# Letting either addition of a bundle run on GpSimd, in a kernel whose exponentials are shared by two engines

## The chip, the cores and the metric

The kernel runs on one core of a Trainium2 chip. The time is device microseconds of that core. The median before is 694.38 us.

## The reference

Two attention blocks read the same input x (2048 x 512) and their outputs are mixed by a gate. Block A is softmax attention with 32 heads of width 16, block B is linear attention with the feature map phi. Each has a fused weight for Q, K, V and an output weight.

```python
def _A_ref(x, wqkv, wo):
    ...
    scores = jnp.einsum("bhqd,bhkd->bhqk", q, k) * (Dh ** -0.5)
    p = _softmax(scores, axis=-1)
    o = jnp.einsum("bhqk,bhkd->bhqd", p, v)
    ...
def _B_ref(x, wqkv, wo):
    ...
    phi = lambda t: jnp.where(t > 0, t + 1, jnp.exp(t)) + 1e-6
    pq, pk = phi(q), phi(k)
    kv = jnp.einsum("bhsd,bhse->bhde", pk, v)
    ...
g = _sigmoid((x * gate_w).sum(-1, keepdims=True))
return g * a + (1 - g) * b
```

Block A needs 32 x 2048 x 2048 exponentials. They are most of the work.

## The kernel before

**Units and rounds.** Block A is cut into 32 rounds (`rounds`): a group of eight heads, a chunk of 512 queries, and one half of the eight heads. A round has 64 units (`NU`). A unit is one head, 128 keys and 512 queries: one matmul of scores into one PSUM bank (128 x 512), the exponential of it, and then the product of the exponentials with V, which is summed in an accumulator bank over the round.

**Two ways to an exponential.** ScalarE takes two or three units at a time (an instruction of 128 x 1024 or 128 x 1536, L2021) and writes bf16 to the tile PT. Or a unit is *claimed* (`claim`): VectorE evicts the scores (L1536), scaling and adding a bias so that the 16-bit integer it writes, read as a float16, is a piecewise linear exponential. To make that precise, three versions of it are summed, whose integers differ by the constants `STEPS` (0, 342, 683). So four claimed units form a *bundle* (`NTRI` = 4): their four evictions go to one buffer of the tile DP (`NB` = 13 buffers, 128 x 2048 each), and when it is full it is closed (`close_tri`, `try_close`): two *additions* of a constant to the whole buffer write the second and the third version to two further buffers. TensorE then makes three products for a claimed unit, with V scaled by a weight, where a ScalarE unit takes one.

**Who adds.** An addition on VectorE is a 16-bit add of a scalar (L1586). On GpSimd it is a 32-bit add of a constant held twice in 32 bits (L1579, the constant in the tile `step`). Only the second addition of a bundle (`z == NG4 - 1`) is given to GpSimd, and only if the bundle is full, all of one round, that round is the one ScalarE is in and isn't the last, and over `POOL_LEFT` = 22 of its units are unclaimed. Which engine an addition uses is fixed when it is queued. Before a GpSimd addition is issued, a VectorE addition must have been issued since the last one (`last_add`, `boost`), and the GpSimd addition waits for its result by a semaphore (`sync`).

**The plan.** All instructions are put in order by a planner written in Python, which runs when the kernel is built. It keeps an estimated time for each engine and estimated ready times of each buffer. VectorE's waiting work is a list of items with priorities (0 and 1 for evictions and most others, 3 for additions). `pump` picks the next one for VectorE, `pool_go` offers items to GpSimd, and `est_start` says when an operation could begin; for a VectorE operation that doesn't read PSUM it adds the times in which GpSimd is expected to run (`pool_runs`). On the chip each engine simply runs its list in order, with semaphores between dependent instructions.

**What decides on a claim.** After each group of scores the planner claims a unit if a PSUM bank is free, a buffer is free (`can_claim`), and the work that waits for VectorE (`dve_load`) is under 3.7 to 4 us. In a group of scores the third bank goes to a claimed unit if one can be claimed, or else, if it is free, to ScalarE as a third unit. While a closed bundle lacks buffers for its additions, the start of another is held back (`MOST_OPEN` = 0).

**Around it.** Projections, block B and the output are *steps* with a target, a count of exponential groups (`cur_g`: units given to ScalarE, divided by three). Targets are multiples of `GPR`, groups a round. TensorE fills idle time with matmuls on a constant tile (`fill`) where its share of useful work falls below `MAC_LOW`.

Of the kernel before, what the change touches and what calls it, by code (L numbers as in the profile page):

```python
# [9 lines left out]
ALU = mybir.AluOpType  # L10
# [3 lines left out]
I32 = mybir.dt.int32  # L14
I16 = mybir.dt.int16
U16 = mybir.dt.uint16

STATS = {}
# [12 lines left out]
STEPS = (0, 342, 683)  # L31
NG4 = len(STEPS)
# [172 lines left out]
def d_sb(n, rate=1.0):  # L205
    return 0.15 + n * 1.042e-3 * rate
# [6 lines left out]
def bass_gated_mix__mha_block__linear_attn_block__prompt_kernel(  # L213
# [27 lines left out]
    pairs_ = [(t8, qc) for t8 in range(NT8 - 2) for qc in range(NQC)] + LAST_ORDER  # L241
    KV0, KV1 = 1.0, 1.2
    PRE_T = 5
    PRE_GAP = 8
    OUT_GAP = 4

    with ExitStack() as es:
        _cnt = [0]

        def SB(shape, dt, name):  # L250
            _cnt[0] += 1
            return es.enter_context(nc.sbuf_tensor(f"{name}_{_cnt[0]}", list(shape), dt))
# [48 lines left out]
        NTU = 512 * NTRI  # L301

        DP = SB([128, NB, NTU], BF16, "DP")
# [5 lines left out]
        rbc = SB([128, 512], FP32, "rbc")  # L309
        dev = SB([128, 2, 128], FP32, "dev")  # L310
        flag = SB([128, 1], I32, "flag")
        step2 = SB([128, 2], I16, "step")
        epool = SB([128, 2, 512], BF16, "epool")
        KVbd = SB([128, NCC, 128], BF16, "KVbd")
        Zsel = SB([128, NCC, 8], BF16, "Zsel")
# [37 lines left out]
        DV = _Eng("dve", SEM("s_dve"))  # L353
# [44 lines left out]
        r_step = R("step")  # L398
# [19 lines left out]
        def est_start(E, reads, writes):  # L418
            t = E.t
            for res in list(reads) + list(writes):  # L420
                if res.we is not E:
                    t = max(t, res.tw + LAT)
                elif not E.ordered:
                    t = max(t, res.tw + SELF_T)
            for res in writes:
                t = max(t, res.tr + LAT)
            if E is DV and not any(res in r_bank for res in reads):
                for a, b in pool_runs:
                    if a <= t < b:
                        STATS["blk"] = STATS.get("blk", 0) + b - t  # L430
                        t = b
            return t

        pool_runs = collections.deque(maxlen=4)
        POOL_SOON = 0.3
        POOL_PASS = 1.0
        last_add = [[], False]
        boost = [False]
        POOL_TT = 1.3
        POOL_V = 0.9  # L440
        POOL_ADD = 1.97
        EVERY = 1
        POOL_LEFT = 22
        OT_POOL = 1
        V2_POOL = 0

# [16 lines left out]
        def blocked(it, reads, writes):  # L463
            return blocker(it, reads, writes) is not None

        def emit_item_op(it, sync=[]):
            fn, reads, writes, dur, after, *on_pool = it.ops.popleft()
            for res in reads:
                res.pend -= 1
            for res in writes:  # L470
                res.pend -= 1
                res.pw -= 1
            if not it.ops:
                items.remove(it)
            if on_pool:
                _emit(PO, fn, reads + sync, writes, on_pool[0])
                pool_runs.append((PO.t - on_pool[0] + 0.08, PO.t + 0.08))
            else:
                _emit(DV, fn, reads, writes, dur)
            if after is not None:  # L480
                after()

        def pool_go(sync=None):

            for it in sorted(items, key=lambda i: i.seq):
                o = it.ops[0]
                if len(o) > 5 and not blocked(it, o[1], o[2]) and est_start(PO, o[1], o[2]) <= DV.t + POOL_SOON:
                    if not last_add[1] and any(x.prio == 3 and len(x.ops[0]) == 5 and not blocked(x, x.ops[0][1], x.ops[0][2])
                                               for x in items):
                        boost[0] = True  # L490
                        return
                    boost[0] = last_add[1] = False
                    STATS["pool"] = STATS.get("pool", 0) + 1
                    emit_item_op(it, last_add[0])
                    return

        def settle(reads, writes):
# [51 lines left out]
        def due_now(it):  # L549
            return of_round.get(it.seq, NR) <= acc_round[0] < act_round[0]  # L550

        def pump(now, look=0.25):
            try_close()
            pool_go()
            while items and DV.t <= now + look:
                best = None
                for it in items:
                    o = it.ops[0]
                    if len(o) > 5 or blocked(it, o[1], o[2]):
                        continue  # L560
                    st = est_start(DV, o[1], o[2])
                    wait = st - DV.t
                    key = (wait > (WAIT_BANK if it.prio <= 1 else 0.12), -1 if it.prio == 3 and (boost[0] or (RUSH and it.ops[0][5:] == () and due_now(it))) else it.prio, st, it.seq)
# [6 lines left out]
                emit_item_op(best[1])  # L570
                pool_go()

        def dve_load(now):
            return max(0.0, DV.t - now) + sum(o[3] for it in items for o in it.ops)

        def flush_items():
            while items:
# [135 lines left out]
        op(PO, lambda: nc.gpsimd.memset(step2[:], STEPS[2]), writes=[r_step], dur=0.1)  # L713
        op(PO, lambda: nc.gpsimd.memset(identb[:], 0.0), writes=[r_ident])
        op(PO, lambda: nc.gpsimd.affine_select(out=identb[:], in_=identb[:], compare_op=ALU.not_equal,
                                               fill=1.0, base=0, pattern=[[-1, 128]], channel_multiplier=1),
# [770 lines left out]
            return r + 1  # L1487

        MIN_LEFT = 14
        MIN_LEFT_LAST = 18  # L1490

        def can_claim(now, js):

# [58 lines left out]
        LAZY = 1  # L1552
        EARLY_ADDS = 1
        MOST_ADDS = 20
        MOST_OPEN = 0
        CLAIM_FREE_OPEN = 2

        def try_close():

            while closing:  # L1560
                i, us, zs = closing[0]
                z = len(zs) + 1
                if z == NG4:
# [12 lines left out]
                mine_, out_ = r_DP[i][0:len(us)], r_DP[i2][0:len(us)]  # L1576
                if (EVERY and z == NG4 - 1 and n == NTU and ntri[0] % EVERY == 0 and us[0][0] == us[-1][0] < NR - 1
                        and us[0][0] == act_round[0] and NU - len(taken[us[0][0]]) > POOL_LEFT):
                    push(3, [(lambda z=z, i2=i2, y=DP[:, i, 0:n].bitcast(I32), n=n: nc.gpsimd.tensor_tensor(  # L1579
                        DP[:, i2, 0:n].bitcast(I32), y, step2[:].bitcast(I32).to_broadcast([128, n // 2]), ALU.add),  # L1580
                        mine_ + [r_step], out_, 0.0, None, POOL_ADD)])
                else:
                    def added(out_=out_):
                        last_add[:] = [out_, True]
                        boost[0] = False
                    push(3, [(lambda z=z, i2=i2, y=y, n=n: nc.vector.tensor_single_scalar(DP[:, i2, 0:n].bitcast(I16), y, STEPS[z], ALU.add),  # L1586
                              mine_, out_, d_sb(n, 0.25), added)])
                of_round[iseq[0]] = us[0][0]
                for k, (r, u) in enumerate(us):
                    add_products(i2, z, k, r, u)  # L1590
            return True


        Q_OFF = -4
        GPR = 15.2
        B0 = 0.8
        B1 = 21
        chains = []

# [213 lines left out]
        FILL_AHEAD = 0.9  # L1813
# [499 lines left out]
```

## Time and profile before

| | |
|---|---|
| median of 3 runs | 694.38 us (693.92 to 694.49) |
| the profiled execution | 693.24 us, of which the span is 691.4 us |
| ScalarE busy | 677.6 us, 98% of the span |
| TensorE busy | 670.5 us, 97% |
| VectorE busy | 624.7 us, 90% |
| GpSimd busy | 249.6 us, 36% |
| granted TensorE clock | 1.000 |

In the rows below PE is TensorE, ACT ScalarE, DVE VectorE, POOL GpSimd, PEld TensorE's weight loads. A row of a group has the line, the engine, the operation, what it writes and reads, shapes and count; then the busy time in us and the mean duration in ns; then the engine's idle time before these instructions and what ended it. A row of the timeline has the start and the duration in us. In a row of a table by stretches, each engine has its busy time and, in brackets, its number of instructions. Neighbouring instructions of one engine overlap a little, so a group's busy time is less than its count times its mean.

### The profile page before, as it was taken

The numbers are of one execution on the slowest core, as the hardware profiler recorded it, in microseconds if no ns is written. First come the engines' busy times: TensorE is split into PE (matmuls) and PEld (weight loads), VectorE is DVE, ScalarE is ACT, GpSimd is POOL, SyncE is SP. The second block draws the span as 40 slices with busy tenths as digits, with TensorE's granted clock in tenths as the row PEclk, the third lists the DMA queues.
The fourth block names the chain that finished last, engine by engine and source line by source line (L and its number), as shares of the span: only waits on it lengthen the run. The fifth ranks groups of instructions, "written<-read, shape, count | busy, mean of one in ns | idle before, by whom it ended". The sixth has DMA issues, their size and how long they took to land.

```text
span 691.4 us, 19104 instructions
## 1 busy us (share of the span) xinstructions
PE 670.5 (97%) x8082; PEld 203.0 (29%) x8084; DVE 624.7 (90%) x1066; ACT 677.6 (98%) x718; POOL 249.6 (36%) x148
## 2 busy tenths in 40 slices
PE   8999999999999999999999999999999999999997
PEld 4322222333223322333232223233222322222223
DVE  4699999898888996998999999999999999999995
ACT  6999999999999999999999999999999999999996
POOL 4033434533235342343323444444334343334400
PEclk9999999999999999999999999999999999999999
DMA  9800101010010012100002010010201201010111
GB/s 228 233 3 14 21 2 32 4 24 13 1 34 3 14 21 63 34 2 18 18 14 51 1 29 15 11 33 11 39 18 23 54 21 41 18 34 24 35 28 46
DMA packets 44815, 22.95 MB, mean 33 GB/s; under 512 B 33976, under 2 KB 40568, under 8 KB 44728
## 3 DMA queue, kind: packets, MB, share of 16 engines
q1 hardware_dynamic: 42712, 20.12, 12.9%
q10 hardware_dynamic: 2016, 1.57, 0.8%
q8 instruction: 66, 1.08, 0.7%
q14 instruction: 21, 0.17, 0.1%
HBM read 8.00 MB, written 2.10 MB: 15 GB/s over the span
## 4 chain that ended last, share of the span: by engine, by line
ACT 80%; PE 15%; DVE 4%; issue 0%; POOL 0%; ACTq 0%; POOLq 0%
ACT PT L2021 78%; PE ps L664 15%; ACT epool L948 2%; DVE DP L1536 2%; DVE DP L1586 1%; DVE epool L951 0%; DVE DP L2123 0%; DVE oraw L1277 0%; DVE xT L1881 0%; DVE phi L953 0%; DVE KT L837 0%; PE ps L671 0%; DVE OB L1076 0%; DVE DP L2128 0%; DVE flag L2133 0%
## 5 line engine op out<-in xcount | busy, mean ns | idle before, releaser
L2021 ACT ACTIVATE PT<-ps 128x1024 bf16<-128x1024 f32 (+1 forms) x678 | 666.5, 1216 | 1.8 <-PE ps L664 1.4
L1536 DVE TENSOR_SCALAR DP<-ps 128x512 int16<-128x512 f32 x612 | 401.7, 683 | 38.1 <-PE ps L664 34.5
L1579 POOL TENSOR_TENSOR DP<-DP,step 128x1024 int32<-128x1024 int32 x116 | 225.9, 1947 | 349.2 <-DVE DP L1586 220.0
L664 PE MATMUL ps<-Qpad,KT 32*128 32x512 bf16 x2048 | 273.7, 384 | 12.7 <-ACT PT L2021 8.2
L664 PE MATMUL ps<-DP,Vaug 128*32 128x512 f16 x1831 | 199.9, 384 | 1.3 <-DVE oraw L1277 0.9
L664 PE MATMUL ps<-PT,Vaug 128*32 128x512 bf16 x1425 | 176.3, 385 | 1.0 <-DVE Vaug L892 0.5
L664 PEld LDWEIGHTS ps<-Qpad,KT 32*128 32x128 bf16 x2048 | 68.6, 91 | 278.8 <-ACT PT L2021 250.5
L1586 DVE TENSOR_SCALAR DP<-DP 128x2048 int16<-128x2048 int16 x190 | 127.4, 686 | 0.2
L664 PEld LDWEIGHTS ps<-DP,Vaug 128*32 128x32 bf16 x1831 | 48.4, 94 | 65.1 <-issue 37.7
L664 PEld LDWEIGHTS ps<-PT,Vaug 128*32 128x32 bf16 x1425 | 41.6, 94 | 54.0 <-issue 40.5
L664 PE MATMUL ps<-warm 128*32 128x512 bf16 (+1 forms) x381 | 56.3, 385 | 1.1 <-POOL step L713 1.1
L1265 POOL TENSOR_TENSOR OT<-oraw,rbc 128x512 bf16<-128x512 f32 x12 | 15.3, 1274 | 56.4 <-DMA rbc<-oraw 28.6
L664 PE MATMUL ps<-xT,wA 128*32 128x512 bf16 x432 | 32.7, 384 | 0.0
L948 ACT ACTIVATE epool<-ps 128x512 bf16<-128x512 f32 x32 | 24.2, 756 | 0.0
L1277 DVE COPY oraw<-ps 128x512 f32<-128x512 f32 x31 | 21.1, 681 | 0.6 <-PE ps L664 0.5
L664 PE MATMUL ps<-wB,xT 128*32 128x512 bf16 x256 | 19.1, 384 | 0.1
L664 PE MATMUL ps<-xT,wB 128*32 128x512 bf16 x256 | 19.1, 383 | 0.0
L664 PEld LDWEIGHTS ps<-warm 128*32 128x32 bf16 (+1 forms) x381 | 14.3, 97 | 15.0 <-issue 12.0
L664 PE MATMUL ps<-woA,OT 128*32 128x512 bf16 (+1 forms) x226 | 18.6, 383 | 0.0
L837 DVE CAST KT<-ps 128x512 bf16<-128x512 f32 (+1 forms) x16 | 10.7, 667 | 6.3 <-PE ps L664 6.3
L953 DVE SCALAR_TENSOR_TENSOR phi<-ps,epool 128x512 bf16<-128x512 f32 x24 | 16.2, 675 | 0.0
L664 PE MATMUL ps<-wA,xT 128*128 128x128 bf16 x192 | 14.5, 220 | 0.0
(106 smaller groups left out, 242.8 us busy)
## 6 DMA issues: line engine op xcount, KB each, us to landing
rbc<-oraw SPq DMA_DIRECT2D x16, 256.0 KB
OT<-in_A_x_dram SPq DMA_DIRECT2D x4, 512.0 KB, 7.2
Qpad<-Qs SPq DMA_DIRECT2D x124, 16.0 KB, 1.8
oraw<-oraw SPq DMA_DIRECT2D x60, 32.0 KB, 1.9
wA<-in_A_wqkv_dram SPq DMA_DIRECT2D x1, 1536.0 KB, 7.6
wB<-in_B_wqkv_dram SPq DMA_DIRECT2D x1, 1536.0 KB, 8.5
out_dram<-outt SPq DMA_DIRECT2D x12, 128.0 KB, 1.7
phi<-in_A_x_dram ACTq DMA_DIRECT2D x3, 256.0 KB, 6.3
```

The source lines that it names most:

```text
L664: return lambda: nc.tensor.matmul(o, lhsT=l, rhs=r, start=start, stop=stop, skip_group_check=sg)
L837: push(1, [(lambda: nc.vector.tensor_copy(KT[:, par, c0:c1], src), [r_bank[b]], [r_KT[par][t]], d_psum(n), None)])
L948: op(AC, lambda: nc.scalar.activation(epool[:, s, :], bank_ap(b), ACT.Exp), reads=[r_bank[b]], writes=[r_e[s]], dur=0.6, issue=0.48)
L953: (lambda: nc.vector.scalar_tensor_tensor(out=dst, in0=bank_ap(b), scalar=0.0, in1=epool[:, s, :], op0=ALU.max, op1=ALU.add), [r_bank[b], ...
L1265: push(1, [(lambda: (nc.gpsimd if on_pool else nc.vector).tensor_tensor(OT[:, t8, 512 * qc:512 * (qc + 1)], oraw[:, 0, :], rbc[:], ALU.mul ...
L1277: push(0, [(lambda: nc.vector.tensor_copy(oraw[:, half, :], acc), [r_acc], [r_oraw[half]], d_psum(512), evicted)])
L1536: push(0 if in_group else 1, [(lambda: nc.vector.tensor_scalar(DP[:, i, 512 * k:512 * (k + 1)].bitcast(I16), bank_ap(b), FRAC - Y_BIAS4, Y ...
L1579: push(3, [(lambda z=z, i2=i2, y=DP[:, i, 0:n].bitcast(I32), n=n: nc.gpsimd.tensor_tensor(DP[:, i2, 0:n].bitcast(I32), y, step2[:].bitcast ...
L1586: push(3, [(lambda z=z, i2=i2, y=y, n=n: nc.vector.tensor_single_scalar(DP[:, i2, 0:n].bitcast(I16), y, STEPS[z], ALU.add), mine_, out_, d ...
L2021: op(AC, lambda p0=p0, b0=b0, n=n: nc.scalar.activation(PT[:, 512 * p0:512 * p0 + n], ps[:, 512 * b0:512 * b0 + n], ACT.Exp, scale=LN2 / F ...
```

## The change

Any addition of a full bundle may now run on either engine, and the choice falls when it is issued. The tile of constants holds both. `pool_go` offers such an addition to GpSimd unless it is due (`due_now`: ScalarE has left its round and the products have reached it), and stands back if GpSimd has run until lately (`YIELD`) and VectorE has another operation on SBUF that could start at once. `pump` lets VectorE take one that isn't due only if GpSimd is occupied for `POOL_WAIT` = 0.7 us more. `port_free` makes GpSimd's estimated start wait for VectorE's last operation on SBUF; the semaphore wait (`sync`) is gone. A waiting addition counts with 0.4 of its duration in VectorE's load (`ADD_W`). With `MOST_OPEN` = 1 a new bundle may be opened while one closed bundle still lacks buffers. Ten numbers of the plan are changed too.

```diff
-    PRE_GAP = 8
+    PRE_GAP = 5
...
-        step2 = SB([128, 2], I16, "step")
+        steps = SB([128, 4], I16, "step")
...
+            elif E is PO:
+                t = max(t, port_free[0])
             return t
...
+        POOL_WAIT = 0.7
+        port_free = [0.0]
+        boost = [None]
+        ADD_W = 0.4
+        YIELD = 1.2
+        YIELD_SOON = 0.2
...
-        def emit_item_op(it, sync=[]):
+        def emit_item_op(it, pool=None):
...
-            if on_pool:
-                _emit(PO, fn, reads + sync, writes, on_pool[0])
+            if len(other) > 1 and pool is None:
+                pool = est_start(PO, reads, writes) + other[0] < est_start(DV, reads, writes) + dur
+            if other and (len(other) == 1 or pool):
...
+                _emit(PO, fn, reads, writes, other[0])
...
             else:
+                if not any(res in r_bank for res in reads):
+                    port_free[0] = est_start(DV, reads, writes) + dur - 0.03
                 _emit(DV, fn, reads, writes, dur)
...
-                    if not last_add[1] and any(x.prio == 3 and len(x.ops[0]) == 5 and not blocked(x, x.ops[0][1], x.ops[0][2])
-                                               for x in items):
-                        boost[0] = True
+                    if len(o) > 6 and due_now(it):
+                        continue
+                    if boost[0] is None and PO.t > DV.t - YIELD:
+                        boost[0] = next((x for x in items if not any(res in r_bank for res in x.ops[0][1]) and len(x.ops[0]) != 6 and x is not it
+                                         and (len(x.ops[0]) == 5 or due_now(x)) and not blocked(x, x.ops[0][1], x.ops[0][2])
+                                         and est_start(DV, x.ops[0][1], x.ops[0][2]) <= DV.t + YIELD_SOON), None)
+                    if boost[0] is not None:
                         return
...
-                    if len(o) > 5 or blocked(it, o[1], o[2]):
+                    if len(o) == 6 or blocked(it, o[1], o[2]):
+                        continue
+                    if len(o) > 6 and not due_now(it) and PO.t < DV.t + POOL_WAIT:
                         continue
...
-            return max(0.0, DV.t - now) + sum(o[3] for it in items for o in it.ops)
+            return max(0.0, DV.t - now) + sum(o[3] * (ADD_W if len(o) > 6 else 1) for it in items for o in it.ops)
...
-        op(PO, lambda: nc.gpsimd.memset(step2[:], STEPS[2]), writes=[r_step], dur=0.1)
+        for z in range(1, NG4):
+            op(PO, lambda z=z: nc.gpsimd.memset(steps[:, 2 * z - 2:2 * z], STEPS[z]), writes=[r_step], dur=0.1)
...
-        MIN_LEFT_LAST = 18
+        MIN_LEFT_LAST = 20
...
-        MOST_OPEN = 0
+        MOST_OPEN = 1
...
+                ops = (lambda z=z, i2=i2, y=y, n=n: nc.vector.tensor_single_scalar(DP[:, i2, 0:n].bitcast(I16), y, STEPS[z], ALU.add),
+                       mine_, out_, d_sb(n, 0.25), None)
+                if n == NTU:
+                    ops = (ops[0], mine_ + [r_step], out_, ops[3], None, POOL_ADD, lambda z=z, i2=i2, y=DP[:, i, 0:n].bitcast(I32), n=n: nc.gpsimd.tensor_tensor(
+                        DP[:, i2, 0:n].bitcast(I32), y, steps[:, 2 * z - 2:2 * z].bitcast(I32).to_broadcast([128, n // 2]), ALU.add))
+                push(3, [ops])
...
-        Q_OFF = -4
-        GPR = 15.2
-        B0 = 0.8
+        Q_OFF = 0
+        GPR = 14.8
+        B0 = 0.4
...
-        OVER = 0.12
+        OVER = 0.15
...
-        MAC_LOW = 0.45
+        MAC_LOW = 0.43
...
-        LATE = 7
+        LATE = 8
```

More of the change, by code (lines that the diff above doesn't have):

```diff
@@ L435, in bass_gated_mix__mha_block__linear_attn_block__prompt_kernel @@
         POOL_SOON = 0.3
-        POOL_PASS = 1.0
-        last_add = [[], False]
-        boost = [False]
+        POOL_WAIT = 0.7
[4 more added lines that the diff above has]
+        YIELD_SOON = 0.2
         POOL_TT = 1.3
@@ L441, in bass_gated_mix__mha_block__linear_attn_block__prompt_kernel @@
         POOL_ADD = 1.97
-        EVERY = 1
-        POOL_LEFT = 22
         OT_POOL = 1
@@ L464, in blocked @@
             return blocker(it, reads, writes) is not None
-        def emit_item_op(it, sync=[]):
-            fn, reads, writes, dur, after, *on_pool = it.ops.popleft()
+        def emit_item_op(it, pool=None):
+            fn, reads, writes, dur, after, *other = it.ops.popleft()
             for res in reads:
@@ L474, in emit_item_op, with pool_go @@
                 items.remove(it)
-            if on_pool:
-                _emit(PO, fn, reads + sync, writes, on_pool[0])
-                pool_runs.append((PO.t - on_pool[0] + 0.08, PO.t + 0.08))
-            else:
+            if len(other) > 1 and pool is None:
+                pool = est_start(PO, reads, writes) + other[0] < est_start(DV, reads, writes) + dur
+            if other and (len(other) == 1 or pool):
+                if len(other) > 1:
+                    fn = other[1]
+                    STATS["pool"] = STATS.get("pool", 0) + 1
+                _emit(PO, fn, reads, writes, other[0])
+                pool_runs.append((PO.t - other[0] + 0.08, PO.t + 0.08))
+            else:
+                if not any(res in r_bank for res in reads):
+                    port_free[0] = est_start(DV, reads, writes) + dur - 0.03
                 _emit(DV, fn, reads, writes, dur)
+            if it is boost[0]:
+                boost[0] = None
             if after is not None:
                 after()
-        def pool_go(sync=None):
+        def pool_go():
             for it in sorted(items, key=lambda i: i.seq):
@@ L487, in pool_go @@
                 if len(o) > 5 and not blocked(it, o[1], o[2]) and est_start(PO, o[1], o[2]) <= DV.t + POOL_SOON:
-                    if not last_add[1] and any(x.prio == 3 and len(x.ops[0]) == 5 and not blocked(x, x.ops[0][1], x.ops[0][2])
-                                               for x in items):
-                        boost[0] = True
+                    if len(o) > 6 and due_now(it):
[5 more added lines that the diff above has]
+                    if boost[0] is not None:
                         return
-                    boost[0] = last_add[1] = False
-                    STATS["pool"] = STATS.get("pool", 0) + 1
-                    emit_item_op(it, last_add[0])
+                    emit_item_op(it, True)
                     return
@@ L562, in pump @@
                     wait = st - DV.t
-                    key = (wait > (WAIT_BANK if it.prio <= 1 else 0.12), -1 if it.prio == 3 and (boost[0] or (RUSH and it.ops[0][5:] == () and due_now(it))) else it.prio, st, it.seq)
+                    key = (wait > (WAIT_BANK if it.prio <= 1 else 0.12), -1 if it is boost[0] else it.prio, st, it.seq)
                     if best is None or key < best[0]:
@@ L569, in pump @@
                     return
-                emit_item_op(best[1])
+                emit_item_op(best[1], False)
                 pool_go()
         def dve_load(now):
-            return max(0.0, DV.t - now) + sum(o[3] for it in items for o in it.ops)
+            return max(0.0, DV.t - now) + sum(o[3] * (ADD_W if len(o) > 6 else 1) for it in items for o in it.ops)
         def flush_items():
@@ L1576, in try_close @@
                 mine_, out_ = r_DP[i][0:len(us)], r_DP[i2][0:len(us)]
[L1577 to L1587, printed above, removed]
+                ops = (lambda z=z, i2=i2, y=y, n=n: nc.vector.tensor_single_scalar(DP[:, i2, 0:n].bitcast(I16), y, STEPS[z], ALU.add),
[4 more added lines that the diff above has]
+                push(3, [ops])
                 of_round[iseq[0]] = us[0][0]
```

## The prediction, made before the change was run

> **What bounds the kernel now.** I read the page first: busy shares, then the chain that ended last.
>
> ```profile
> PE 670.5 (97%) x8082; PEld 203.0 (29%) x8084; DVE 624.7 (90%) x1066; ACT 677.6 (98%) x718; POOL 249.6 (36%) x148
> ...
> ACT 80%; PE 15%; DVE 4%; issue 0%; POOL 0%; ACTq 0%; POOLq 0%
> ```
>
> ScalarE is busy through 98% of a span of 691.4 us and holds 80% of the chain. So the time is the number of exponentials that ScalarE computes itself, times what one costs. Every unit that VectorE claims is one fewer for ScalarE. The groups of instructions, with shapes kept apart, give both prices:
>
> ```profile
> L2021 ACT ACTIVATE PT<-ps 128x1024 bf16<-128x1024 f32 x598 | 568.0, 1167 | 1.1 <-PE ps L664 0.9
> L2021 ACT ACTIVATE PT<-ps 128x1536 bf16<-128x1536 f32 x80 | 118.9, 1585 | 0.7 <-PE ps L664 0.5
> ...
> L1536 DVE TENSOR_SCALAR DP<-ps 128x512 int16<-128x512 f32 x612 | 401.7, 683 | 38.1 <-PE ps L664 34.5
> L1586 DVE TENSOR_SCALAR DP<-DP 128x2048 int16<-128x2048 int16 x190 | 127.4, 686 | 0.2
> ...
> L1579 POOL TENSOR_TENSOR DP<-DP,step 128x1024 int32<-128x1024 int32 x116 | 225.9, 1947 | 349.2 <-DVE DP L1586 220.0 <-DVE DP L1536 129.1
> L1265 POOL TENSOR_TENSOR OT<-oraw,rbc 128x512 bf16<-128x512 f32 x12 | 15.3, 1274 | 56.4 <-DMA rbc<-oraw 28.6 <-DVE DP L1586 14.4 <-DVE Vaug L892 5.8
> ```
>
> 598 x 2 + 80 x 3 = 1436 units on ScalarE, 612 on VectorE, together the 2048 of 32 rounds. 612 units are 153 bundles of four, with 306 additions: 190 on VectorE, 116 on GpSimd. One unit costs ScalarE 568.0 / 1196 = 0.475 us. It costs VectorE 401.7 / 612 = 0.656 us for the eviction, and an addition 127.4 / 190 = 0.671 us. The eviction row shows VectorE's only large wait, 38.1 us. To see whether VectorE is full where it matters I read the timeline:
>
> ```profile
> 106.79 1.32 DVE L1536 TENSOR_SCALAR DP<-ps 128x512 int16<-128x512 f32 x2
> 108.03 0.68 DVE L869 TENSOR_SCALAR Qs<-ps 128x512 bf16<-128x512 f32 x1
> 108.63 1.32 DVE L1536 TENSOR_SCALAR DP<-ps 128x512 int16<-128x512 f32 x2
> 109.86 0.34 DVE L1250 RECIPROCAL rraw<-rsum 128x32 f32<-128x32 f32 x1
> 110.17 0.69 DVE L1536 TENSOR_SCALAR DP<-ps 128x512 int16<-128x512 f32 x1
> 110.78 0.68 DVE L1586 TENSOR_SCALAR DP<-DP 128x2048 int16<-128x2048 int16 x1
> ```
>
> No gap stands between these rows. So ScalarE and VectorE are full together, and the split between them sets the time. The 80 three-wide exponentials say the same: outside the start, ScalarE takes a third unit when a bank was free and no claim could be made. GpSimd is the engine with room, 36% busy.
>
> **The change, part by part.**
>
> *How many additions can move.* Today only the second addition of a bundle goes to GpSimd, under five conditions, and it waits for a VectorE addition. Afterwards either may go. The timeline of GpSimd shows the room (first and last of 128 rows from 40 us on):
>
> ```profile
> 40.09 1.89 POOL L1579 TENSOR_TENSOR DP<-DP,step 128x1024 int32<-128x1024 int32 x1 [30.48 <-DVE DP L1536]
> 43.75 1.89 POOL L1579 TENSOR_TENSOR DP<-DP,step 128x1024 int32<-128x1024 int32 x1 [1.77 <-DVE DP L1586]
> ...
> 654.41 1.89 POOL L1579 TENSOR_TENSOR DP<-DP,step 128x1024 int32<-128x1024 int32 x1 [1.98 <-DVE DP L1586]
> ```
>
> The last number of each row is the idle time before it. Cutting each of the 127 gaps after the first into pieces of 2.2 us (1.947 for an addition, the rest my allowance for the handover) gives 100 whole pieces. The least that can move is none, the most about 100. I take half, 50, so 166 on GpSimd: a gap can be used only if an addition is ready in it, additions of a round that is due stay on VectorE, and GpSimd lets VectorE's own memory operations go first. The ends are kept for the range.
>
> *What a moved addition is worth.* 50 x 0.671 = 33.5 us of VectorE. It becomes time only through more claims. One more bundle takes 4 x 0.475 = 1.90 us from ScalarE. It costs VectorE 4 x 0.656 = 2.62 and, with the number on GpSimd held, two additions, 1.34. As the whole gets 1.90 us shorter, VectorE also has 0.90 x 1.90 = 1.71 us less to work in. Together 5.68 us of VectorE a bundle. 33.5 / 5.68 = 5.9 bundles, 11.2 us, before anything is lost.
>
> *The port.* The ready-made wait of GpSimd's addition for a VectorE addition goes; afterwards only the plan's estimated times keep the two apart. Three places of the timeline price a meeting, and the last two rows give the least, median and longest duration of each kind of addition:
>
> ```profile
> 207.84 1.27 POOL L1265 TENSOR_TENSOR OT<-oraw,rbc 128x512 bf16<-128x512 f32 x1 [4.69 <-DMA rbc<-oraw]
> 208.23 1.42 DVE L1586 TENSOR_SCALAR DP<-DP 128x2048 int16<-128x2048 int16 x1
> ...
> 163.45 1.28 DVE L1586 TENSOR_SCALAR DP<-DP 128x2048 int16<-128x2048 int16 x2
> 164.21 2.27 POOL L1579 TENSOR_TENSOR DP<-DP,step 128x1024 int32<-128x1024 int32 x1 [3.65 <-DVE DP L1586]
> ...
> 357.18 1.89 POOL L1579 TENSOR_TENSOR DP<-DP,step 128x1024 int32<-128x1024 int32 x1 [10.04 <-DVE DP L1586]
> 357.62 0.68 DVE L869 TENSOR_SCALAR Qs<-ps 128x512 bf16<-128x512 f32 x1
> 358.22 1.36 DVE L1536 TENSOR_SCALAR DP<-ps 128x512 int16<-128x512 f32 x2
> ...
> L1586 DVE TENSOR_SCALAR DP<-DP x190: 628/682/1424, 34.1 to 677.2; 128x2048 int16<-128x2048 int16 x190
> L1579 POOL TENSOR_TENSOR DP<-DP,step x116: 1891/1892/2399, 40.1 to 654.4; 128x1024 int32<-128x1024 int32 x116
> ```
>
> A VectorE addition that begins 0.39 us into a GpSimd operation takes 1.42 us, 0.74 above its median of 0.682. A GpSimd addition that meets one of VectorE takes 2.27 instead of 1.892. Evictions from PSUM run beside GpSimd at their usual 0.68. [...] The mean of VectorE's additions, 686 ns, is only 4 ns above the median, 190 x 0.004 = 0.8 us in all, so about one met GpSimd today. Nothing but the plan held VectorE's additions behind GpSimd's there, so the plan can do it. With GpSimd half as busy again and no wait from the other side I put 8 of the 140 left at 0.74 us, 5.9 us. The ends are none, and half of them (a rival below).
>
> 33.5 - 5.9 = 27.6; / 5.68 = 4.86 bundles (19 units); x 1.90 = 9.2 us gained.
>
> *What else those 19 claims load.* A claimed unit needs three products on TensorE where ScalarE's needs one, plus nothing for the scores, which both need.
>
> ```profile
> L664 PE MATMUL ps<-DP,Vaug 128*32 128x512 f16 x1831 | 199.9, 384 | 1.3 <-DVE oraw L1277 0.9
> ...
> 30.00:680.00 650.00, 50.71 (x364) 12.68 (x360) 0.00 (x0) 1.00 0.11 23
> ```
>
> 199.9 / 1831 = 0.109 us a product; 19 x 2 x 0.109 = 4.1 us more, in 9.2 us less time, 13.3 us. The second row is the matmuls on the constant tile that only fill idle TensorE time, 50.71 us between 30 and 680 us: the cover. Without it the 4.1 would be paid in full.
>
> *Buffers.* An addition on GpSimd holds its tiles 1.892 - 0.682 = 1.2 us longer, and there are 13 tiles, three for a bundle. That a bundle may now open while another still lacks buffers works against this. Bounds: one bundle more or less, -1.9 to +1.9; I take 0.
>
> *GpSimd's queue.* Its 12 normalisations now queue behind more additions, each by up to 1.9 us. They have 56.4 us of idle time before them today, so nobody is shown waiting on them; 0.
>
> *The end.* Today no addition is on GpSimd after 656.3 us. Afterwards one of the last round may be, and TensorE's last products wait for it: 0 to 1.2 us, I take 0.6. The last round stops claiming at 20 units left instead of 18, inside that figure.
>
> *The start and the constants.* One more small fill on GpSimd ahead of the identity:
>
> ```profile
> L713 POOL MEMSET step<- 128x2 int16 x1 | 0.1, 101 | 0.0
> ```
>
> 0 to 0.1 us, hidden behind the arrival of x; 0. The projection steps come due every 14.8 instead of 15.2 exponential groups (a group is three units) a round. With 1436 - 19 = 1417 units a round has 1417 / 96 = 14.8, so nothing comes late by it. The thresholds on TensorE's filling (0.43 for 0.45), overrun and lateness, and the gap of 5 instead of 8 groups between the last pre-sums, shift single steps by a group; bounded by one bundle either way, -1.9 to 1.9, taken as 0.
>
> **The sum.** The profiled execution took 693.24 us. 693.24 - 9.2 + 0.6 = 684.6. The median of the runs shown, 694.38, is 1.14 above it: 685.8. With 24 to 79 additions moved and 4 to 8 meetings, the same arithmetic gives 4.4 to 15.8 us less, so this case alone holds 679 to 691.
>
> **The rivals.**
>
> *GpSimd takes nearly all it can.* 100 moved, none meeting: 67.1 / 5.68 = 11.8 bundles, 22.4 us, with the 0.6 of the end 672.6. For: the new rule offers an addition to GpSimd by default and VectorE may take one that isn't due only when GpSimd is occupied for 0.7 us more. Against: the gaps are partly those in which no bundle was ready, and TensorE's cover, 10.3 + 22.4 us of the 50.71, gets thin.
>
> *VectorE is no longer what holds claims back.* The relief becomes VectorE idle time: the 38.1 us before evictions grows to some 70 and the time stays within 694.4 +- 1.4 (0.2%, about what a measurement of this kernel can tell from no change). For: those 38.1 us are waits for scores, already there. Against: the unbroken rows above.
>
> *The meetings eat the relief: slower.* [...] At 0.74 us each the point of no gain is 33.5 / 0.74 = 45 meetings. With half of the 140 meeting, 51.8 - 33.5 = 18.3 us of VectorE is lost, 3.2 bundles fewer, 6.1 us, with the 0.6 of the end 701.1. For: one real meeting costs more than a whole addition. Against: a single one in 190 today, and the plan counts the port for both engines.
>
> **Chances.** Forecast 0.56, GpSimd takes nearly all 0.16, no change 0.07, slower by meetings 0.21. So faster by over 0.2%: 0.72; within: 0.07; slower: 0.21. The range, 672 to 701, leaves out the far half of the 672.6 case and the far half of the slower one, together just under 0.2.
>
> **What would show it.** GpSimd additions 150 to 200, VectorE additions 110 to 160; evictions about 631; ScalarE units about 1417; VectorE busy share still near 90%. VectorE additions' mean within 40 ns of the median says that the port is kept in turns. Wrong: evictions at 612 or fewer while VectorE's idle time before them grows (no change), or a mean above 0.85 us with maxima near 2 us (meetings).

## The result, and the profile after

The changed kernel takes 747.04 us in the median of four runs (743.66 to 750.69) beside 694.43 us for the kernel before: a ratio of 1.076, 95% interval 1.069 to 1.083. The profiled execution took 743.70 us, its span is 742.0, 50.6 us more than before. The page's busy shares and chain, to be held against those of the prediction:

```profile
PE 678.1 (91%) x7954; PEld 203.0 (27%) x7954; DVE 624.1 (84%) x943; ACT 676.9 (91%) x708; POOL 534.8 (72%) x302
...
PE 42%; ACT 31%; DVE 24%; issue 2%; DMA 1%; POOL 0%; DVEq 0%; ACTq 0%; POOLq 0%
```

ScalarE works for as long as before (676.9 us, 677.6 then) in a longer span. Its share of the chain fell from 80% to 31%, and TensorE and VectorE took it over. The groups, shapes kept apart, say where ScalarE stood still and who was slow:

```profile
L2033 ACT ACTIVATE PT<-ps 128x1024 bf16<-128x1024 f32 x586 | 559.1, 1114 | 49.1 <-PE ps L680 48.2
L2033 ACT ACTIVATE PT<-ps 128x1536 bf16<-128x1536 f32 x81 | 118.2, 1587 | 2.8 <-PE ps L680 2.5
...
L1553 DVE TENSOR_SCALAR DP<-ps 128x512 int16<-128x512 f32 x632 | 412.5, 685 | 70.8 <-PE ps L680 68.1
L1594 DVE TENSOR_SCALAR DP<-DP 128x2048 int16<-128x2048 int16 x47 | 63.1, 1370 | 0.1
L968 DVE TENSOR_SCALAR epool<-epool 128x512 bf16<-128x512 bf16 x32 | 24.5, 772 | 0.3 <-ACT epool L965 0.3
...
L1597 POOL TENSOR_TENSOR DP<-DP,step 128x1024 int32<-128x1024 int32 x269 | 510.6, 1928 | 188.2 <-DVE DP L1553 184.0 <-PE ps L680 4.0
```

ScalarE's idle time before the exponentials is 49.1 + 2.8 = 51.9 us, where it was 1.1 + 0.7 = 1.8. The difference, 50.1, is nearly all of the 50.6 us by which the span grew. It waited for scores from TensorE. The claims came close to the forecast, 632 for 631, and ScalarE has 1416 units left. But VectorE's few remaining additions take 1370 ns each instead of 686, and its small maps on `epool` 772 instead of 354. Their engine wasn't waiting (0.1 and 0.3 us of idle time): the instruction itself was held up. Durations of the two kinds of addition, least, median and longest:

```profile
L1597 POOL TENSOR_TENSOR DP<-DP,step x269: 1882/1892/2396, 32.7 to 727.8; 128x1024 int32<-128x1024 int32 x135
L1594 DVE TENSOR_SCALAR DP<-DP x47: 629/983/2409, 61.9 to 714.1; 128x2048 int16<-128x2048 int16 x47
```

I call *blocked time* what VectorE's operations that don't read PSUM take above the mean of the same shape in the kernel before: 47 x (1370 - 686) ns = 32.1 us for the additions, 32 x (772 - 354) ns = 13.4 for the maps, and 21.5 for small groups like the first two of these rows. The last three rows are the same work in the kernel before.

```profile
L1241 DVE TENSOR_TENSOR dev<-rraw,dev 128x128 f32<-128x128 int32 x6 | 6.8, 1138 | 0.0
...
L1071 DVE TENSOR_TENSOR rdB<-rdB,gom 128x128 f32<-128x128 f32 x4 | 4.4, 1099 | 0.0
...
L951 DVE TENSOR_SCALAR epool<-epool 128x512 bf16<-128x512 bf16 x32 | 11.3, 354 | 0.4
...
L1224 DVE TENSOR_TENSOR dev<-rraw,dev 128x128 f32<-128x128 int32 x6 | 1.6, 272 | 0.0
...
L1054 DVE TENSOR_TENSOR rdB<-rdB,gom 128x128 f32<-128x128 f32 x4 | 1.1, 280 | 0.0
```

Together 67.0 us. The list of waits shows how it spreads. VectorE's late evictions (L1553) and its late additions (L1594), whose results the products need, hold TensorE. TensorE's late scores hold ScalarE.

```profile
DVE DP L1553 <- PE ps L680: 68.1, 184, 2.2
ACT PT L2033 <- PE ps L680: 50.7, 65, 3.5
PE ps L680 <- DVE DP L1553: 18.4, 22, 2.5
PEld ps L680 <- DVE DP L1594: 14.9, 12, 3.0
PE ps L680 <- DVE DP L1594: 12.6, 13, 2.7
```

One place of the timeline holds the whole story:

```profile
59.04 8.34 POOL L1597 TENSOR_TENSOR DP<-DP,step 128x1024 int32<-128x1024 int32 x4 [3.15 <-DVE DP L1553]
...
61.87 3.77 DVE L1594 TENSOR_SCALAR DP<-DP 128x2048 int16<-128x2048 int16 x2
65.56 0.68 DVE L886 TENSOR_SCALAR Qs<-ps 128x512 bf16<-128x512 f32 x1
...
57.31 7.53 ACT L2033 ACTIVATE PT<-ps 128x1024 bf16<-128x1024 f32 x7
66.45 1.02 ACT L2033 ACTIVATE PT<-ps 128x1024 bf16<-128x1024 f32 x1 [1.61 <-PE ps L680]
...
65.69 0.39 PE L680 MATMUL ps<-DP,Vaug 128*32 128x512 f16 x1 [1.69 <-DVE DP L1594]
66.01 0.39 PE L680 MATMUL ps<-Qpad,KT 32*128 32x512 bf16 x3
```

GpSimd starts four additions in a row as soon as their bundles are evicted. Two VectorE additions then take 3.77 us instead of about 1.28. TensorE stands idle for 1.69 us in front of a product that needs the second one, and only behind that product come the next scores (the row with `Qpad,KT`). ScalarE has run out of scores at 64.84 and stands idle for 1.61 us.

### The profile page after: what moved, and what is told of

It reads as the page before. It is cut to its first block, busy times and chain, and to the rows that moved or that the text cites. A ratio compares the mean times of both kernels' runs of the same rounds, so it can differ in the third digit from the quotient of the medians.

```text
span 742.0 us, 18872 instructions
## 1 busy us (share of the span) xinstructions
PE 678.1 (91%) x7954; PEld 203.0 (27%) x7954; DVE 624.1 (84%) x943; ACT 676.9 (91%) x708; POOL 534.8 (72%) x302
## 4 chain that ended last, share of the span: by engine, by line
PE 42%; ACT 31%; DVE 24%; issue 2%; DMA 1%; POOL 0%; DVEq 0%; ACTq 0%; POOLq 0%
PE ps L680 42%; ACT PT L2033 30%; DVE DP L1553 9%; DVE DP L1594 6%; DVE epool L968 3%; DVE Vaug L920 1%; DVE dev L1241 1%; DVE oraw L1294 1%; DVE rdB L1071 1%; ACT epool L965 1%; DVE Vaug L909 1%; DMA rsum<-oraw 1%; DVE phi L970 1%; DVE KT L854 0%; DVE Qs L886 0%
## 5 line engine op out<-in xcount | busy, mean ns | idle before, releaser
L2033 ACT ACTIVATE PT<-ps 128x1024 bf16<-128x1024 f32 (+1 forms) x668 | 661.8, 1171 | 51.9 <-PE ps L680 50.7
L1597 POOL TENSOR_TENSOR DP<-DP,step 128x1024 int32<-128x1024 int32 x269 | 510.6, 1928 | 188.2 <-DVE DP L1553 184.0
L1553 DVE TENSOR_SCALAR DP<-ps 128x512 int16<-128x512 f32 x632 | 412.5, 685 | 70.8 <-PE ps L680 68.1
L680 PE MATMUL ps<-Qpad,KT 32*128 32x512 bf16 x2048 | 280.5, 392 | 33.8 <-DVE DP L1553 14.9
L680 PE MATMUL ps<-DP,Vaug 128*32 128x512 f16 x1884 | 196.8, 390 | 14.3 <-DVE DP L1594 12.6
L680 PE MATMUL ps<-PT,Vaug 128*32 128x512 bf16 x1406 | 167.2, 396 | 0.8 <-DVE Vaug L909 0.5
L1594 DVE TENSOR_SCALAR DP<-DP 128x2048 int16<-128x2048 int16 x47 | 63.1, 1370 | 0.1
L680 PE MATMUL ps<-warm 128*32 128x512 bf16 (+2 forms) x193 | 31.4, 408 | 1.1 <-POOL step L730 1.1
L968 DVE TENSOR_SCALAR epool<-epool 128x512 bf16<-128x512 bf16 x32 | 24.5, 772 | 0.3 <-ACT epool L965 0.3
L965 ACT ACTIVATE epool<-ps 128x512 bf16<-128x512 f32 x32 | 20.9, 653 | 0.0
```

The costliest lines, as they stand in the source:

```text
L680: return lambda: nc.tensor.matmul(o, lhsT=l, rhs=r, start=start, stop=stop, skip_group_check=sg)
L965: op(AC, lambda: nc.scalar.activation(epool[:, s, :], bank_ap(b), ACT.Exp), reads=[r_bank[b]], writes=[r_e[s]], dur=0.6, issue=0.48)
L968: (lambda: nc.vector.tensor_scalar(epool[:, s, :], epool[:, s, :], 1.0, 1e-6, op0=ALU.min, op1=ALU.add), [r_e[s]], [r_e[s]], 0.29, None),
L1553: push(0 if in_group else 1, [(lambda: nc.vector.tensor_scalar(DP[:, i, 512 * k:512 * (k + 1)].bitcast(I16), bank_ap(b), FRAC - Y_BIAS4, Y ...
L1594: ops = (lambda z=z, i2=i2, y=y, n=n: nc.vector.tensor_single_scalar(DP[:, i2, 0:n].bitcast(I16), y, STEPS[z], ALU.add), mine_, out_, d_sb ...
L1597: ops = (ops[0], mine_ + [r_step], out_, ops[3], None, POOL_ADD, lambda z=z, i2=i2, y=DP[:, i, 0:n].bitcast(I32), n=n: nc.gpsimd.tensor_te ...
```

## Theories

**Out of turn.** The plan lets GpSimd and VectorE's operations on SBUF take turns at what it calls the port, but after the change no wait holds GpSimd to its turn. GpSimd starts each addition when its data is there, ahead of the VectorE operation that the plan put first. That operation is held up. The evictions queued behind it are late, and so are the products that need its result, the scores that stand behind these products or need the banks, and the exponentials. In the changed kernel 26 of the 47 VectorE additions begin while a GpSimd operation runs; their median is 2.38 us, that of the other 21 is 0.68.

**Rivals.** *Latency*: an addition of 1.9 us gives the products their data too late, whoever holds the port. *Numbers*: the nine other constants, the early opening of a bundle among them, spoil the order.

## Experiments

| kernel | evictions | blocked, us | ScalarE idle before exponentials, us | span, us | median, us (and ratio to before) |
|---|---|---|---|---|---|
| before | 612 | 0 | 1.8 | 691.4 | 693.4 to 694.4 |
| changed | 632 | 67.0 | 51.9 | 742.0 | 747.0 (1.069 to 1.083) |
| changed, with a wait | 632 | 4.1 | 3.0 | 686.8 | 687.6 (0.989 to 0.994) |
| changed, wait on every second | 632 | 24.6 | 10.4 | 695.5 | 697.6 (1.005 to 1.009) |
| changed, wait for additions only | 632 | 34.1 | 29.0 | 716.2 | 717.6 (1.026 to 1.038) |
| before, wait removed | 612 | 50.1 | 37.3 | 734.3 | 734.2 (1.051 to 1.058) |

**A wait added to the changed kernel.** No instruction is moved. A GpSimd operation only waits, in addition, for VectorE's last operation on SBUF that was issued before it.

```diff
+        port_ev = []
...
-                _emit(PO, fn, reads, writes, other[0])
+                _emit(PO, fn, reads, writes, other[0], also=port_ev)
...
             else:
                 if not any(res in r_bank for res in reads):
                     port_free[0] = est_start(DV, reads, writes) + dur - 0.03
-                _emit(DV, fn, reads, writes, dur)
+                    port_ev[:] = [_emit(DV, fn, reads, writes, dur)]
+                else:
+                    _emit(DV, fn, reads, writes, dur)
...
-            ev = E.add(fn, _deps_for(reads, writes), inc=inc)
+            ev = E.add(fn, _deps_for(reads, writes) + list(also), inc=inc)
```

> The changed kernel with one thing more: each GpSimd addition also waits, by a semaphore, for the last VectorE operation on SBUF that the plan issued before it. The instruction lists and their order stay the same on every engine. Theory 'out of turn' (GpSimd additions start earlier than the plan assumes and hold the port while VectorE's short SBUF operations stand in front of evictions): VectorE additions return to a mean under 800 ns (1370 in the changed kernel), ScalarE's idle time before exponentials falls from 51.9 us to under 15, time 680 to 705. Rival 'latency' (an addition of 1.9 us on GpSimd gives the products their data too late, whoever holds the port): additions on GpSimd start no earlier than now, so ScalarE's idle time stays at 50 or more and the time at 740 to 760. Rival 'numbers' (the other constants and the bundle that may open early spoil the order): 740 to 750, as the order is unchanged.

It took 687.62 us, ratio 0.9916 (0.9893 to 0.9939): 59 us faster than the changed kernel and 0.8% faster than the one before. Its groups, two rows of its waits, and the same place of its timeline:

```profile
L1597 DVE TENSOR_SCALAR DP<-DP 128x2048 int16<-128x2048 int16 x47 | 34.5, 761 | 0.1
...
L971 DVE TENSOR_SCALAR epool<-epool 128x512 bf16<-128x512 bf16 x32 | 10.7, 338 | 1.1 <-ACT epool L968 1.0
...
L2036 ACT ACTIVATE PT<-ps 128x1024 bf16<-128x1024 f32 x586 | 559.3, 1212 | 2.3 <-PE ps L683 1.8
...
PE ps L683 <- DVE DP L1556: 2.1, 2, 1.7
...
PE ps L683 <- DVE DP L1597: 0.2, 1, 0.2
```

```profile
62.19 1.28 DVE L1597 TENSOR_SCALAR DP<-DP 128x2048 int16<-128x2048 int16 x2
...
63.55 5.59 POOL L1600 TENSOR_TENSOR DP<-DP,step 128x1024 int32<-128x1024 int32 x3 [5.62 <-DVE DP L1597]
...
57.47 10.44 ACT L2036 ACTIVATE PT<-ps 128x1024 bf16<-128x1024 f32 x10
```

GpSimd now stands idle for 5.62 us, until VectorE's two additions are through in 1.28. ScalarE goes on without a gap. Over the whole run TensorE's matmuls wait 0.2 us for VectorE's additions, where it was 12.6, and 2.1 us for its evictions, where it was 18.4. GpSimd's additions start later than in the changed kernel here, and the kernel is faster, so *latency* falls; the order of the lists is the same, so *numbers* falls as the main cause.

**The kernel before, its wait removed.**

```diff
-                _emit(PO, fn, reads + sync, writes, on_pool[0])
+                _emit(PO, fn, reads + sync, writes, on_pool[0], free=sync)
...
-            ev = E.add(fn, _deps_for(reads, writes), inc=inc)
+            ev = E.add(fn, _deps_for([res for res in reads if res not in free], writes), inc=inc)
```

`sync` still counts in the plan's estimate and no longer in the waits.

> The kernel before, without the wait of its 116 GpSimd additions for the last VectorE addition; nothing else, the lists and their order are the same. Theory 'out of turn': the GpSimd addition starts as soon as its bundle is evicted, before the VectorE addition that the plan put ahead of it; most of the 116 meet one. At 0.7 us each, 116 x 0.7 = 80 us of blocked VectorE time, mean of VectorE additions 900 to 1150 ns, time 710 to 745. Rivals 'latency' and 'numbers': no change or slightly faster, as additions end earlier: 690 to 696, mean of VectorE additions within 40 ns of 686.

Its groups of both kinds of addition:

```profile
L1586 DVE TENSOR_SCALAR DP<-DP 128x2048 int16<-128x2048 int16 x190 | 170.6, 913 | 0.2
...
L1579 POOL TENSOR_TENSOR DP<-DP,step 128x1024 int32<-128x1024 int32 x116 | 244.0, 2104 | 380.6 <-DVE DP L1536 380.5
```

734.15 us, ratio 1.0548 (1.0514 to 1.0582), with identical lists: time and mean as *out of turn* expected, blocked time 50.1 us where I had put 80. That so few additions met GpSimd in the kernel before was the work of its wait, not of its plan. GpSimd's additions suffer too, at a mean of 2104 ns for 1947. The one that begins second is late in the traces. Each of the 26 VectorE additions of the changed kernel that begin inside a GpSimd operation ends 0.55 us behind it. The other way round, in the kernel before with its wait, 16 GpSimd additions begin 0.52 to 0.65 us ahead of the end of a VectorE addition and take 2.27 to 2.40 us; the other 100 take 1.89.

**Other doses.** With the wait on every second GpSimd addition:

> The changed kernel with the added wait on every second GpSimd addition only; lists and order as in the changed kernel. Theory 'out of turn': the loss goes with the additions that may still start early, so between the two: 700 to 732, and the time lost against 687.6 within 15 us of the VectorE time blocked (the excess of VectorE's SBUF operations over their usual durations). Rival 'one stall starts a train' (a single early addition upsets the order for long): near the changed kernel, 735 to 750. Rival 'a wait anywhere re-aligns the engines': near 688 to 695.

697.61 us, less than the 700 to 732 that *out of turn* gave and more than the 688 to 695 of a wait that re-aligns the engines. There are 20.5 us more blocked time than with all waits and 8.7 us more span. So half of the waits prevents far more than half of the loss; why is not shown. With the wait for VectorE's additions only, not for its other operations on SBUF:

> The changed kernel with the added wait only for VectorE's additions, not for its other SBUF operations (the maps epool, V's scaling, the checks dev, rdB, reciprocals). If the loss comes from additions alone (33 of some 68 us of blocked time): 687 to 695. If the short operations matter as their blocked time says (about 35 us of 68): 700 to 720, epool's mean staying over 600 ns while additions fall under 850.

717.55 us. Here 30.0 us more blocked time than with all waits cost 29.4 us, and nearly all of it is in the short operations: epool's mean is 805 ns, the additions' 790. So the half of the loss that doesn't come from additions is real. Per us of blocked time the span grew by 0.42 us (every second), 1.0 (additions only), 0.88 (the changed kernel against the one with all waits: 55.2 for 62.9) and 0.86 (42.9 for 50.1 in the kernel before).

**A wait in both directions.** VectorE's operations on SBUF also wait for the GpSimd operation put before them. The lines are given against the kernel with the one wait:

```diff
+        pool_ev = []
...
-                _emit(PO, fn, reads, writes, other[0], also=port_ev)
+                pool_ev[:] = [_emit(PO, fn, reads, writes, other[0], also=port_ev)]
...
-                    port_ev[:] = [_emit(DV, fn, reads, writes, dur)]
+                    port_ev[:] = [_emit(DV, fn, reads, writes, dur, also=pool_ev)]
```

> The changed kernel with the wait in both directions: VectorE's operations on SBUF also wait, by a semaphore, for the GpSimd operation that the plan put before them. If the order of GpSimd's starts was the whole fault, the second wait adds nothing, as the port makes the later one wait anyway: 684 to 691, within 3 us of the kernel with one wait. If meetings that are left there (a VectorE addition of 2.1 us) still cost: under 683. If semaphores themselves cost time: over 691.

Only the last of the three expectations has the side, and none the size: 735.78 us, ratio 1.0635 (1.0587 to 1.0683). Now no VectorE operation is blocked (additions at 689 ns), but the list of waits shows that waiting for GpSimd by a semaphore does the same harm:

```profile
DVE DP L1598 <- POOL DP L1601: 37.9, 23, 2.0
ACT PT L2037 <- PE ps L684: 36.1, 44, 2.0
```

So it isn't the plan's order as such that has to be kept, and the port isn't the cost as such. What costs is VectorE standing still in front of its evictions and additions, at the port or at a semaphore. The wait helps because it makes GpSimd the one that stands back, and leaves VectorE free to go first when GpSimd is late.

**Only the second addition may go to GpSimd**, in the changed kernel without a wait (`if n == NTU and z == NG4 - 1`).

> The changed kernel, but only the second addition of a bundle may go to GpSimd; the first is VectorE's. Theory 'out of turn': fewer GpSimd additions (at most 160 instead of 269) but more VectorE additions that can meet them (150 instead of 47), still with no wait: 720 to 770, VectorE additions' mean over 900 ns. Rival 'latency': half of the late data is gone, 705 to 725. Rival 'numbers': 735 to 750.

786.01 us, ratio 1.136 (1.128 to 1.145), slower even than the 720 to 770 of *out of turn*. Fewer additions on GpSimd (158), yet slower: 158 VectorE additions are there to be held up, at a mean of 1136 ns, and blocked time is 78.2 us. *Latency* expected this one to be faster.

**The old numbers**, in the changed kernel without and with the wait (`PRE_GAP`, `MIN_LEFT_LAST`, `MOST_OPEN`, `Q_OFF`, `GPR`, `B0`, `OVER`, `MAC_LOW`, `LATE` as before: nine numbers, not ten as I counted).

> The changed kernel with the ten numbers of the plan set back, among them the one that lets a bundle open while another lacks buffers. Theory 'out of turn': within 10 us of the changed kernel, 737 to 757, VectorE additions' mean over 1100 ns. Rival 'numbers': 685 to 710. Rival 'latency': 740 to 755.

> The changed kernel with the added wait and the ten numbers of before. Theory 'out of turn': the numbers matter little once the order is kept, 684 to 694. Rival 'numbers' (the new ones are worse in themselves): under 683. Rival 'numbers are needed' (the new ones and the early opening make the gain): 692 to 700.

Without the wait 719.42 to 737.90 us, a spread too wide for a ratio, and nearly all of it below the 737 to 757 that I expected. In the profiled execution, the fastest, blocked time is 50.4 us; its lists are not those of the changed kernel. The 685 to 710 of *numbers* are not reached. With it 687.00, ratio 0.9911 (0.9894 to 0.9927), the same as with the new numbers. Once VectorE goes first, neither the numbers nor the early opening of a bundle matter to the time.

**What a moved addition is worth.** The changed kernel with no addition on GpSimd (`if False`):

> The changed kernel, its numbers kept, with all additions on VectorE. It measures what a moved addition is worth. By the prediction's rate (5.68 us of VectorE a bundle, 1.90 us of ScalarE): 116 x 0.671 / 5.68 = 13.7 bundles fewer than before, 26 us more, 715 to 725. If VectorE's time is only partly what holds claims back: 698 to 712. In both cases faster than the changed kernel.

705.93 us, ratio 1.0183 (1.0166 to 1.0200). So the changed kernel, with 269 additions taken off VectorE, is 41 us slower than with none. Its VectorE is full, and claims are fewer:

```profile
L1553 DVE TENSOR_SCALAR DP<-ps 128x512 int16<-128x512 f32 x581 | 383.4, 684 | 14.9 <-PE ps L680 10.5
L1594 DVE TENSOR_SCALAR DP<-DP 128x2048 int16<-128x2048 int16 x290 | 195.4, 689 | 0.0
```

The kernel before, with its old numbers, has 116 additions on GpSimd, and against this one they bring 31 claims and 12.6 us; the next 153 (269 with the wait) bring 20 claims and 5.9 us, while VectorE's idle time before evictions goes from 14.9 over 38.1 to 74.2 us. So moving additions from VectorE to GpSimd helps here, 18 us in all (687.6 us for 705.9), if VectorE goes first, and hurts if not (747.0).

**Buffers**, 12 and 14 for 13, with the wait.

> The changed kernel with the added wait and 12 buffers for bundles instead of 13. Once the port is kept in turns, VectorE stands idle 74 us before evictions, so something else holds claims back. If it is the buffers, one fewer costs at least 12 claims: evictions under 620, time 692 to 702. If it is the scores and banks on TensorE's side, nearly nothing: evictions 626 to 634, 686 to 690.

> The same with 14 buffers. If buffers hold claims back, evictions 640 or more and 676 to 684. If they don't at this number: evictions 626 to 636, 684 to 691.

691.07 us with 616 evictions, and 689.16 with 631. One buffer fewer costs 3.5 us, just below the 692 I gave that case; one more brings nothing. At 13 the buffers are no longer what holds claims back. What does was not found.

**The clock.** TensorE's granted clock fell to 0.97 on average, and in one stretch of the changed kernel (the column after POOL) to 0.85:

```profile
480.00:530.00 50.00, 44.65 (x544) 13.45 (x544) 45.30 (x73) 47.27 (x52) 36.10 (x20) 1.00 0.13 24
530.00:580.00 50.00, 42.92 (x438) 12.17 (x442) 42.47 (x63) 39.05 (x43) 33.44 (x19) 0.85 0.12 25
```

> The changed kernel (without the added wait) with the two thresholds below which TensorE is filled with matmuls on the constant tile raised from 0.43 and 0.45 to 0.7. It asks how much of the loss is the granted clock, which fell to 0.97 on average and 0.85 in one stretch. If TensorE's stalls lower the clock and the clock makes a good part of the loss (among the four runs of the changed kernel 0.960 goes with 750.5 us and 0.970 with 743.7): clock 0.985 or more and 725 to 738. If the clock is a mere by-product: 740 to 755 whatever the clock. The fill can stand only where the plan sees TensorE idle, so the clock may also stay where it is; then this run tells nothing on it.

775.58 us, ratio 1.118 (1.115 to 1.122), at a clock of 0.936, outside both of the ranges given. It tells nothing on the clock: there is 68.9 us of blocked time as in the changed kernel, but more matmuls stand in TensorE's list (285 on the constant tile for 193), and the clock fell further. With the wait the clock is 0.997 with the same lists, so it fell with the stalls. The trace of the changed kernel says more. The clock stands at one half in ten spells, and at full speed between them. The first begins at 66.8 us, behind the stall shown in the timeline above. Here is one of them, and the sum of all ten:

```profile
575.40:585.70 10.30, 9.27 (x62) 2.49 (x62) 8.68 (x14) 6.14 (x6) 7.15 (x6) 0.50 0.19 38
...
sum 44.60, PE 42.65 PEld 9.10 DVE 32.23 ACT 26.90 POOL 13.24; mean PE 4.26 PEld 0.91 DVE 3.22 ACT 2.69 POOL 1.32
```

ScalarE is idle for 44.6 - 26.9 = 17.7 us in them. In the whole span it is idle for 65.1 us, 51.3 more than before. So at least 33.6 of these 51.3 us lie at the full clock, which speaks against the clock as the main part of the loss. How large its part is stays open.

## Why the prediction was wrong

The step that failed is *the port*: "Nothing but the plan held VectorE's additions behind GpSimd's there, so the plan can do it", and from it 8 meetings at 0.74 us, 5.9 us. Measured: 67.0 us. There are four faults in it.

- The count of meetings. The near-absence of meetings in the kernel before was credited to the plan, though the text itself names the wait that goes. The same kernel without it has 50.1 us of blocked time.
- The price of one. 0.74 us came from the only meeting among the additions, in which GpSimd had begun 0.39 us earlier with a short operation. Against an addition of 1.89 us a VectorE addition takes up to 2.41 us. The trace of the kernel before had a dearer meeting, which I overlooked because I looked at additions alone: a map that takes 0.28 us in most cases took 2.04 us there, beginning 0.01 us behind a GpSimd addition.

```profile
64.28 1.89 POOL L1579 TENSOR_TENSOR DP<-DP,step 128x1024 int32<-128x1024 int32 x1 [2.27 <-DVE DP L1536]
64.29 2.04 DVE L951 TENSOR_SCALAR epool<-epool 128x512 bf16<-128x512 bf16 x1
```

- The kinds. I counted additions alone. Half of the blocked time, 35 of 67 us, is in the maps, checks and scalings.
- The exchange. I let lost VectorE time lower the claims, 1.90 us for 5.68. But the lists are fixed when the kernel is built, and the plan doesn't see what the port does. Claims stayed at 632, and lost time went into ScalarE's idle time, at 0.88 us of span for one of blocked time.

The rival "the meetings eat the relief" had the meetings and even the sign to look for (a mean above 0.85 us, maxima near 2 us), but 701 us for 747, above all by the last fault, and a chance of 0.21. That its 51.8 us of blocked time came near the 67.0 is partly luck: it let 70 of 140 additions be met at 0.74 us, where 47 were left.

The other steps. *Additions that move*: 269 for 166, above even my upper end of 216. I had let half of the pieces of 2.2 us be used, but GpSimd runs its additions back to back, four in 7.49 us, and the same gaps cut into pieces of 1.87 us give 138. *Worth of a moved addition*: too high. 153 x 0.671 / 5.68 = 18 bundles, 34 us; with the wait it was 5 bundles and 5.9 us. The rival "VectorE is no longer what holds claims back" was right in this: its idle time grew to 74.2 us. *Claims and units*: 632 and 1416 for 631 and 1417, but by luck: more additions moved and each was worth less. *Constants*: within the bounds given, 687.0 us with the old and 687.6 with the new ones, both with the wait. *Buffers*: one more brings nothing, so a shortage doesn't show. *GpSimd's queue* and *the end*: no run isolates them. *ScalarE's unit as the price of time*: right only as long as ScalarE never waits.

## What to carry to other kernels

A plan that models a shared resource moves nothing on the chip: where the order of two engines matters as it did here, put a semaphore on the engine that can afford to stand back, and none on the one with a queue of urgent work, as 687.6 us with the one wait and 735.8 with both say here. A resource that shows no conflict in a trace may be protected by the very wait that a change removes; removing that wait alone, before the rest, shows it, as 50.1 us of blocked time in the kernel before did here. Time lost where a fixed plan can't see it cost 0.4 to 1.0 us a us here, while VectorE time that the plan knew of was traded at far less: 153 additions, 103 us by the prediction's 0.671, for 5.9 us.

## What the runs showed of the hardware that I had not expected

Not all of VectorE's operations on SBUF were held up by GpSimd here. In the changed kernel reciprocals from SBUF to SBUF keep their time (means of 346 ns for 342 and 932 for 944), although 13 of the 15 small ones begin while a GpSimd operation runs. Tensor-scalar and two-input operations on SBUF grow two- to fourfold in most groups: additions from 686 to 1370 ns, maps on `epool` from 354 to 772, the 128x128 groups on `dev` from 272 to 1138 and on `rdB` from 280 to 1099. The reciprocals of the changed kernel, then those of the one before:

```profile
L1267 DVE RECIPROCAL rraw<-rsum 128x32 f32<-128x32 f32 x15 | 5.2, 346 | 5.1 <-DMA rsum<-oraw 5.1
...
L1070 DVE RECIPROCAL rdB<-rdB 128x128 f32<-128x128 f32 x4 | 3.7, 932 | 0.0
...
L1250 DVE RECIPROCAL rraw<-rsum 128x32 f32<-128x32 f32 x15 | 5.1, 342 | 0.0
L1053 DVE RECIPROCAL rdB<-rdB 128x128 f32<-128x128 f32 x4 | 3.8, 944 | 0.0
```

The plan treats every operation that doesn't read PSUM as a user of the port, these too.
